# A fused gated attention and SwiGLU kernel: pieces of h ahead of other loads, one store behind them, and another mix of work slots

## Chip, cores and metric

The kernel runs on one NeuronCore of a Trainium2 chip. TensorE (PE) multiplies matrices, ScalarE (ACT) applies functions, VectorE (DVE) and GpSimd (POOL) work element by element, and SyncE (SP) issues most DMAs. The engines run beside one another and wait for each other by semaphores; each of them, and SP's queue of DMA issues, works through its own list in the order in which the program wrote it. The metric is the device time of one execution in microseconds; a smaller one is better. The kernel before takes 1419.05 us, the median of 3 runs (1418.94 to 1419.2).

## The reference

All arrays are float32; x has 2048 rows of 512. Attention has 32 heads of 16 columns, and the SwiGLU part an inner width of 1792. A sigmoid of one number per row mixes the two results.

```python
g = sigmoid((x * gate_w).sum(-1, keepdims=True))
# a: attention
q, k, v = (x @ wqkv) split into 32 heads of 16
p = softmax(q k^T / 4)               # 2048 x 2048 for each head
a = (p v, heads side by side) @ wo
# b: SwiGLU
h = silu(x @ w1) * (x @ w3)          # 2048 x 1792
b = h @ w2
out = g * a + (1 - g) * b
```

## The kernel before

**Products in three parts.** A float32 operand is split into a high part in the format fp32r and a low part that holds the rest. A product is the sum of high by high, high by low and low by high. The splitting is a cast and a subtraction: for weights and for h both are done by GpSimd (`halves_of`, lines 483 to 489), which reads a loaded tile ("fr" or "sg") and writes a pair of tiles. Such a call is one DMA on SP's queue and two GpSimd instructions. There are three "fr" buffers, three "raw", two each of "sg", "fh1", "fl1", "fh3" and "fl3", one "gw" and one "hx".

**Prologue and end.** The prologue turns x round, makes v for all rows and the first quarter of q and k, and takes about 85 us. At the end, behind the main loop, the last heads are divided by their sums and the second half of the output is made.

**The main loop** (lines 762 to 788) reads a string of letters, written ahead of time, and writes one piece of work for each letter. TensorE runs them in this order.
- *Q*: the scores of one unit, which is 128 keys by 512 queries for two heads (two matmuls of 512 columns, lines 736 to 747), and behind them the exp on ScalarE, of 128 x 1024 elements, into one of 8 tiles p. The scores have two buffers, so a Q slot can start only when ScalarE has read the scores of the Q slot two before it. 1024 Q slots in all.
- *P*: p by v for two units, eight matmuls of 512 columns (line 730).
- *F*: `feed`, which is filler: one matmul in each half of the array, for two blocks of other work at once (lines 409, 521 and 607 are the three kinds). A block that has run its matmuls in one half of the array runs them again in the other.

A *long* period (`one`) is eight Q, 20 F and four P, with the four P in one run at its end. A *short* period (`two`) is eight Q, 14 F and four P in two runs of two, with two Q between the runs. The string is 99 long periods, one lead-over, and 29 short ones, the last of which is cut at its end.

**The filler's blocks** come from `blocks` (lines 640 to 656) in this order: the other three quarters of q and k, and then w1 and w3 products for 14 slices f of h with four row blocks b each (136 blocks of 24 half slots, which make 1632 F slots); then h by w2 for 16 row tiles t (48 blocks of 28 half slots); then the output projection of the first six row tiles. The last two slices of h, f = 12 and 13, are taken in the order (12, 0), (12, 1), (13, 0), (13, 1), (12, 2), (13, 2), (12, 3), (13, 3). What the loop does not place is run behind it (line 798).

**h.** After a w1 product (`gate_done`) its result is copied, and ScalarE's exp of it is written at the next Q slot ahead of a P. The rest of the sigmoid, a sum, eight reciprocals of 64 columns and the final product, goes to a list `small`, of which each Q slot writes one or two steps on VectorE. The final product (`product`, lines 456 to 463) also stores the block to `h_d` in DRAM. For the w2 products h is read back by row tile: `load_piece(t, q)` (lines 497 to 503) reads rows 4q to 4q + 3 of slices for the 128 columns of tile t and splits them. Tile t has four pieces, q = 0 to 3, the last half as long; from t = 2 on a piece is written when its predecessor of tile t - 2 has been used for the last time. The w2 blocks (`load_w2`, lines 491 to 495) take the place of x in SBUF: block f goes to tiles that a row block of x had, so its cast waits until the last w1 and w3 products of that row block are done. w2 blocks 12 and 13 take the place of the last row block.

**The list `loads`** holds calls of `load_w2` and of `load_piece` for t = 0 and 1. A Q slot takes one of them, every second Q slot as long as `hurry` is false (which it is until the last w3 product), and each one after that (lines 779 and 780). As a slice is finished, calls are put at the list's end; the order in it is the order on SP's queue and on GpSimd:

```python
if f == NF - 1 and b == 0:
    loads.extend([lambda q=q: load_piece(0, q) for q in range(2)])
...
if (f, b) == (NF - 2, NB - 1):
    loads.extend([lambda q=q: load_piece(0, q) for q in (2, 3)])
if f == NF - 1:
    loads.extend([lambda c=c: load_w2(c) for c in range(4 * b, min(4 * b + 4, NF))])
```

Of the kernel before, what the change touches and what calls it, by code (L numbers as in the profile page):

```python
# [17 lines left out]
P = 128  # L18
# [5 lines left out]
NB = S // 512  # L24
NT = S // P
ND = D // P
NF = F // P
# [6 lines left out]
def gated_mix_kernel(ctx: ExitStack, tc: tile.TileContext, x, wqkv, wo, w1, w3, w2, gate_w, out):  # L34
# [18 lines left out]
    nc = tc.nc  # L53
# [16 lines left out]
    h_d = dram.tile([F, S], F32, name="h_d")  # L70
# [10 lines left out]
    def slot(tag, dtype=F32R, shape=(P, 512)):  # L81

        return (fw if tag[0] == "f" else fk).tile(list(shape), dtype, name=tag, bufs=BUFS.get(tag, 2))
# [185 lines left out]
    def load_step(s):  # L269
        half, j = divmod(s, NPAIR)  # L270
        load_q(j, half, s % 2)
        load_k(j, s % 2)
        load_guard(j, half, s % 2)
# [36 lines left out]
    def load_weights(chunk):  # L310
        out = []
        for n, w in zip("13", chunk["src"]):
# [5 lines left out]
            else:  # L318
# [7 lines left out]
    chunks = [dict(src=(wqkv[:, P * c:P * c + P], wqkv[:, D + P * c:D + P * c + P]), first=c == 1)  # L326
              for c in range(1, ND)]
# [74 lines left out]
    soon, later, small, stages, loads = [], [], [], [], []  # L402
    hurry = False
# [44 lines left out]
    def up_done(f, b):  # L448
        def done(ps):
            nonlocal hurry  # L450
            st = state[b]
            assert all(o["gone"] for o in state.values() if o is not st and o["last"])
            sg, gu = st["sg"], slot("hx" if st["last"] else "raw", F32)
            nc.vector.tensor_mul(gu, ps, st["gs"])

            def product():
                st["gone"] = True
                nc.vector.tensor_mul(sg, gu, sg)
                nc.sync.dma_start(h_d[P * f:P * f + P, 512 * b:512 * b + 512], sg)
                if f == NF - 1 and b == 0:  # L460
                    loads.extend([lambda q=q: load_piece(0, q) for q in range(2)])
                if f == NF - 1 and b == NB - 1:
                    loads.extend([lambda q=q: load_piece(1, q) for q in (2, 3)])

            if st["exp"]:
                small.append(product)
            else:
                st["up"] = product
            if (f, b) == (NF - 2, NB - 1):
                loads.extend([lambda q=q: load_piece(0, q) for q in (2, 3)])  # L470
            if f == NF - 1:
                loads.extend([lambda c=c: load_w2(c) for c in range(4 * b, min(4 * b + 4, NF))])
                if b == NB - 1:
                    loads.extend([lambda q=q: load_piece(1, q) for q in range(2)])
                    hurry = True
        return done
# [6 lines left out]
    def halves_of(src, hi, lo, tag):  # L483

        r = slot(tag, F32)
        n = hi.shape[-1]
        nc.sync.dma_start(r[:, 0:n] if len(src.shape) == 2 else r[:, 0:n].rearrange("p (f t) -> p f t", t=P), src)
        nc.gpsimd.tensor_copy(hi, r[:, 0:n])  # L488
        nc.gpsimd.tensor_sub(lo, r[:, 0:n], hi)  # L489

    def load_w2(f):
        if f % 4 == 0:
            w2H.append(xp.tile([P, 4, 512], F32R, name=f"xH{f // 4}"))
            w2L.append(xp.tile([P, 4, 512], F32R, name=f"xL{f // 4}"))
        halves_of(w2[P * f:P * f + P, :], w2H[-1][:, f % 4, :], w2L[-1][:, f % 4, :], "fr")

    def load_piece(t, q):
        hi, lo = (slot(SETS[t % 2][2 * q + i]) for i in range(2))
        tag = "fr" if t == 0 or t == 1 and q < 2 else "sg"
        n = min(4, NF - 4 * q)  # L500
        src = h_d[512 * q:512 * q + P * n, P * t:P * t + P].rearrange("(f p) t -> p f t", p=P)
        halves_of(src, hi[:, 0:P * n], lo[:, 0:P * n], tag)
        hs.setdefault(t, []).append((hi, lo))
# [72 lines left out]
    def divide(k, half):  # L576

        yield from reciprocals(k, half)
        for b in (2 * half, 2 * half + 1):
            for _ in range(5):  # L580
                yield
            if half == 0:
                o, r = slot("hx", F32), slot("gw", F32)
            else:
                both = wk.tile([P, 2, 512], F32, name="od")
                o, r = both[:, 0, :], both[:, 1, :]
            fetch_o(k, b, o, r)
            for _ in range(7):
                yield
            nc.gpsimd.tensor_mul(o, o, r)  # L590
            for _ in range(3):
                yield
            nc.sync.dma_start(N_d[P * k:P * k + P, 512 * b:512 * b + 512], o)
            yield
        if (k, half) == (2, 1):
            load_wo(2)
# [65 lines left out]
    lanes, ready, over = [None, None], ([], []), []  # L662
# [18 lines left out]
    def feed(rest=REST, gap=GAP):  # L681
        did = 0
        for lane in range(2):
            if lanes[lane] is None:
                lanes[lane] = pick(lane, rest, gap)
        for lane in range(2):
            t = lanes[lane]
            if t is None:
                continue
            product, done, length = t["block"]  # L690
            did += 1
            second = t["turn"] is not None
            ins = product(t["ps"], slice(64 * lane, 64 * lane + 64), t["n"], second)
            if second and t["n"] == 0:
                after(ins, t["turn"])
            t["n"] += 1
            if t["n"] == length:
                lanes[lane] = None
                if second:
                    done(t["ps"])  # L700
                    over[t["id"]] = clock
                else:
                    turn = nc.vector.memset(tick[:, 0:1], 0.0)  # L703
                    after(turn, ins)
                    t.update(n=0, turn=turn, since=clock)
                    ready[1 - lane].append(t)
        return did
# [18 lines left out]
    def pv(two):  # L726
        for j, half, k, gq, n, p in two:
            for h in range(2):
                r = 32 * (2 * gq + h)
                nc.tensor.matmul(acc[r:r + DH + 1, :], V[:, k, 2 * j + h, :], p[:, h, :],  # L730
                                 start=k == 0, stop=k == NT - 1)
            free.append(n)
        if k == NT - 1:
            evac(j, half)

    def score(j, half, k, gq):
        i = (NPAIR * half + j) % 2
        ps = psum2()
        t = 512 * gq
        for h in range(2):  # L740
            r = 64 * h
            nc.tensor.matmul(ps[:, h, :], Kt[i][r:r + 50, P * k:P * k + P],  # L742
                             Qt[i][r:r + 50, t:t + 512], start=True, stop=True)
        n = free.pop(0)
        p = wk.tile([P, 2, 512], F32, name=f"p{n}")
        nc.scalar.activation(p, ps, AF.Exp, scale=SCALE)  # L746
        return j, half, k, gq, n, p
# [3 lines left out]


    NP = 8
    LONG, SHORT = 99, 29
    one = "QQFFFFF" + "QFFF" * 5 + "QPPPP"
    two = "QFFF" * 4 + "QFFQPPQQPP"
    order = one * LONG + "QQFFF" + two * (SHORT - 1) + "QFFF" * 4 + "QPPQPP"
    free = list(range(NP))

# [1 line left out]
    pend, issued, clock = [], 0, 0  # L761
    for i, c in enumerate(order):
        clock += 1 if c != "P" else 4
        if c == "Q":
            step = issued // 32 + 1
            if issued % 32 == 6 and step < 2 * NPAIR:
                assert 8 * (ND - 1) - qk_left >= 8 * min(step // 4, ND - 1)
                load_step(step)
            pend.append(score(*next(units)))
            issued += 1  # L770
            while soon and order[i + 1] == "P":
                soon.pop(0)()
            if issued % 128 == (40 if issued // 128 == 5 else 12) and 1 <= issued // 128 < 8:
                stages.append(divide((issued // 128 - 1) % 4, (issued // 128 - 1) // 4))
            if small or later and hurry:
                for _ in range(3 if hurry else 1 + (len(small) > (6 if len(over) < 8 * len(chunks) - 16 else 0))):
                    if small or later and hurry:
                        (small or later).pop(0)()
            if loads and (hurry or issued % 2):
                loads.pop(0)()  # L780
            for stage in stages[:1]:
                if next(stage, stages) is stages:
                    stages.pop(0)
        elif c == "F":
            feed()
        else:
            pv(pend[:2])
            pend = pend[2:]
# [78 lines left out]
```

## Time and profile before

| | before |
|---|---|
| median of 3 runs | 1419.05 us (1418.94 to 1419.2) |
| profiled execution | 1419.72 us |
| its span, first to last instruction | 1417.9 us |
| mean granted TensorE clock | 0.997 |
| TensorE busy | 1407.5 us (99%) |
| ScalarE busy | 1022.8 us (72%) |
| VectorE busy | 484.0 us (34%) |
| GpSimd busy | 318.5 us (22%) |
| 16 DMA engines | 141.44 MB moved, 39.2% busy by SP's queue |

Times in rows of the profile are microseconds from the first instruction, unless marked ns. A row of the timeline has start, length, engine, line, operation, tiles written and read, shape and count; in brackets stand the idle time ahead of it and what ended that. Matmuls are pipelined and their ends are modelled: a row's length is not its price, the distance to the next row's start is. PEld is TensorE's loading of weights, which runs beside its matmuls. A row of the waits has the waiting engine and line, what it waited for, the total, the number of waits and the longest. SPq is SP's queue of DMA issues; a row of it that is long is one that stood and waited. The chain is the work that ended last, followed back from the end.

### The profile page before, as it was taken

Reading aid. Unit: us, or ns where it says so; the run is one execution under the profiler, and the core shown is the slowest. Engines: PE = TensorE matmul, PEld = TensorE weight load, DVE = VectorE, ACT = ScalarE, POOL = GpSimd, SP = SyncE. Lnnn points to the kernel's source line nnn. Section 1 sums busy time; section 2 is a strip of 40 time slices with the busy share of each in tenths; the row PEclk is TensorE's granted clock in tenths of the full one; section 3 lists DMA queues with packets and bytes.
Section 4 is the critical chain, followed back from the end, with each engine's and each line's share of the span. In section 5 each row is a group of like instructions: output and inputs, shape, how many; then the busy total and the mean of one; then the engine's idle time right before and its main releaser. Section 6 shows DMA issues by size and latency. Waiting matters only on the chain.

```text
span 1417.9 us, 28858 instructions
## 1 busy us (share of the span) xinstructions
PE 1407.5 (99%) x11399; PEld 809.7 (57%) x11399; DVE 484.0 (34%) x1067; ACT 1022.8 (72%) x1153; POOL 318.5 (22%) x356
## 2 busy tenths in 40 slices
PE   9999999999999999999999999999999999999998
PEld 7865555555555556555555555555555555555546
DVE  4421111554546445554454544531111101110113
ACT  4547777787777777777777777766777788888880
POOL 5023433110011011101110111553333422223130
PEclk9999999999999999999999999999999999999999
DMA  7554344333213333332233433444443443444435
GB/s 197 145 126 119 117 124 126 92 98 76 60 52 81 88 70 76 78 81 79 53 82 71 106 76 81 120 107 115 116 98 87 110 93 74 96 110 117 99 116 176
DMA packets 112671, 141.44 MB, mean 100 GB/s; under 512 B 16400, under 2 KB 70672, under 8 KB 109456
## 3 DMA queue, kind: packets, MB, share of 16 engines
q1 hardware_dynamic: 110384, 135.72, 39.2%
q10 hardware_dynamic: 2144, 3.80, 0.8%
q8 instruction: 92, 1.51, 0.5%
q14 instruction: 51, 0.42, 0.1%
HBM read 90.70 MB, written 48.76 MB: 98 GB/s over the span
## 4 chain that ended last, share of the span: by engine, by line
PE 93%; POOL 0%; DMA 0%; DVE 0%; issue 0%; ACT 0%; SPq 0%; ACTq 0%; POOLq 0%
PE acc L730 32%; PE f L409 27%; PE S L742 20%; PE f L521 11%; PE f L607 1%; PE f L95 0%; PE f L96 0%; PE f L97 0%; PE S L95 0%; PE S L97 0%; PE S L96 0%; DMA fr<-in_B_w_dram 0%; ACT p L746 0%; POOL xL L489 0%; POOL raw L489 0%
## 5 line engine op out<-in xcount | busy, mean ns | idle before, releaser
L746 ACT ACTIVATE p<-S 128x1024 f32<-128x1024 f32 x1024 | 957.6, 1045 | 319.7 <-PE S L742 319.3
L730 PE MATMUL acc<-p,V 128*17 128x512 f32 x4096 | 470.4, 594 | 0.0
L742 PE MATMUL S<-Qt,Kt 50*128 50x512 f32 x2048 | 414.6, 417 | 1.2 <-SPq L278 0.6
L742 PEld LDWEIGHTS S<-Qt,Kt 50*128 50x128 f32 x2048 | 183.8, 184 | 226.2 <-ACT p L746 85.4
L730 PEld LDWEIGHTS acc<-p,V 128*17 128x17 f32 x4096 | 104.5, 97 | 271.8 <-issue 266.5
L440 DVE RECIPROCAL sg<-sg 128x64 f32<-128x64 f32 x448 | 208.7, 517 | 38.0 <-issue 35.6
L409 PE MATMUL f<-xL,fh 64*128 64x512 f32 x1024 | 205.9, 392 | 0.0
L409 PE MATMUL f<-xH,fh 64*128 64x512 f32 x1024 | 205.8, 392 | 0.0
L409 PE MATMUL f<-xH,fl 64*128 64x512 f32 x1024 | 205.7, 391 | 0.0
L321 POOL CAST fh<-fr 128x512 fp32r<-128x512 f32 x32 | 20.8, 650 | 423.5 <-DMA fr<-in_B_w_dram 374.7
L409 PEld LDWEIGHTS f<-xH,fh 64*128 64x128 f32 x1024 | 98.9, 186 | 16.3
L409 PEld LDWEIGHTS f<-xH,fl 64*128 64x128 f32 x1024 | 98.9, 186 | 16.0
L409 PEld LDWEIGHTS f<-xL,fh 64*128 64x128 f32 x1024 | 98.8, 186 | 16.1
L703 DVE MEMSET tick<- 1x1 f32 x190 | 11.2, 59 | 262.4 <-PE f L521 130.9
L521 PE MATMUL f<-xL,fh 64*128 64x512 f32 x224 | 68.3, 399 | 0.0
L521 PE MATMUL f<-xH,fh 64*128 64x512 f32 x224 | 65.6, 399 | 2.7 <-POOL fh L488 2.7
L521 PE MATMUL f<-xH,fl 64*128 64x512 f32 x224 | 67.0, 399 | 0.0
L432 DVE COPY gs<-f 128x512 f32<-128x512 f32 x56 | 38.6, 689 | 79.9 <-PE f L409 77.7
L540 DVE SCALAR_TENSOR_TENSOR y<-f,omg,y 128x512 f32<-128x512 f32 x32 | 24.1, 752 | 118.1 <-PE f L521 118.1
L438 DVE TENSOR_SCALAR sg<-sg 128x512 f32<-128x512 f32 x56 | 27.8, 496 | 94.6 <-ACT sg L437 93.3
L521 PE MATMUL f<-xH,raw 64*128 64x512 f32 x192 | 58.2, 391 | 0.0
L711 DVE COPY u<-acc 128x512 f32<-128x512 f32 x32 | 22.1, 692 | 92.8 <-PE acc L730 87.3
(217 smaller groups left out, 1353.1 us busy)
## 6 DMA issues: line engine op xcount, KB each, us to landing
Kt<-kH_d SPq DMA_DIRECT2D x128, 128.0 KB
h_d<-sg SPq DMA_DIRECT2D x56, 256.0 KB
sg<-h_d SPq DMA_DIRECT2D x43, 256.0 KB
fr<-in_B_w_dram SPq DMA_DIRECT2D x42, 256.0 KB
Qt<-qH_d SPq DMA_DIRECT2D x128, 64.0 KB
Kt<-kL_d SPq DMA_DIRECT2D x64, 128.0 KB
fr<-in_A_wqkv_dram SPq DMA_DIRECT2D x18, 256.0 KB
Qt<-qL_d SPq DMA_DIRECT2D x64, 64.0 KB
```

The source lines that it names most:

```text
L321: nc.gpsimd.tensor_copy(wh, r)
L409: return nc.tensor.matmul(ps, w[i == 2][r, k, :], (xL if i == 1 else xH)[b][r, k, :], start=n == 0 and not second, stop=n == 3 * ND - 1 an ...
L432: nc.vector.tensor_copy(gs, ps)
L438: small.append(lambda: nc.vector.tensor_scalar(sg, sg, 1.0, None, op0=OP.add))
L440: small.append(lambda q=q: nc.vector.reciprocal(sg[:, q:q + 64], sg[:, q:q + 64]))
L521: ins = nc.tensor.matmul(ps, hs[t][q][i == 2][r, P * o:P * o + P], (w2L if i == 1 else w2H)[q][r, o, :], start=n == 0 and not second, stop ...
L540: nc.vector.scalar_tensor_tensor(y, ps, omg[:, t:t + 1], y, op0=OP.mult, op1=OP.add)
L607: return nc.tensor.matmul(ps, ot[t][i == 2][r, P * k:P * k + P], wo_[k][i == 1][r, :], start=n == 0 and not second, stop=n == 3 * ND - 1 a ...
L711: nc.vector.tensor_copy(u, acc)
L730: nc.tensor.matmul(acc[r:r + DH + 1, :], V[:, k, 2 * j + h, :], p[:, h, :], start=k == 0, stop=k == NT - 1)
L742: nc.tensor.matmul(ps[:, h, :], Kt[i][r:r + 50, P * k:P * k + P], Qt[i][r:r + 50, t:t + 512], start=True, stop=True)
L746: nc.scalar.activation(p, ps, AF.Exp, scale=SCALE)
```

## The change

It has three parts.
- The calls of `load_piece(0, ...)` are put at the front of `loads` and not at its end. The store of the last h block (f = 13, b = 3) is no longer written at once but put at the end of the list; the calls that follow it there, pieces (1, 2) and (1, 3), follow it still.
- From block 125 of the 136 on, each Q slot takes a load from the list, not every second one.
- The string has 78 long periods and 50 short ones in place of 99 and 29. A long period has 21 F, the added one behind the first two Q; a short one has 15 F, the added one ahead of the last Q before the first P run. In all there are 2388 F in place of 2387.

```diff
             def product():
                 st["gone"] = True
                 nc.vector.tensor_mul(sg, gu, sg)
-                nc.sync.dma_start(h_d[P * f:P * f + P, 512 * b:512 * b + 512], sg)
+                store = lambda: nc.sync.dma_start(h_d[P * f:P * f + P, 512 * b:512 * b + 512], sg)
+                if f == NF - 1 and b == NB - 1:
+                    loads.append(store)
+                    loads.extend([lambda q=q: load_piece(1, q) for q in (2, 3)])
+                    return
+                store()
                 if f == NF - 1 and b == 0:
-                    loads.extend([lambda q=q: load_piece(0, q) for q in range(2)])
-                if f == NF - 1 and b == NB - 1:
-                    loads.extend([lambda q=q: load_piece(1, q) for q in (2, 3)])
+                    loads[0:0] = [lambda q=q: load_piece(0, q) for q in range(2)]
...
             if (f, b) == (NF - 2, NB - 1):
-                loads.extend([lambda q=q: load_piece(0, q) for q in (2, 3)])
+                loads[0:0] = [lambda q=q: load_piece(0, q) for q in (2, 3)]
...
-    LONG, SHORT = 99, 29
-    one = "QQFFFFF" + "QFFF" * 5 + "QPPPP"
-    two = "QFFF" * 4 + "QFFQPPQQPP"
+    LONG, SHORT = 78, 50
+    one = "QQFFFFFF" + "QFFF" * 5 + "QPPPP"
+    two = "QFFF" * 5 + "QPPQQPP"
     order = one * LONG + "QQFFF" + two * (SHORT - 1) + "QFFF" * 4 + "QPPQPP"
...
-            if loads and (hurry or issued % 2):
+            if loads and (hurry or issued % 2 or len(over) > 8 * len(chunks) - 12):
                 loads.pop(0)()
```

## The prediction

> **What bounds the kernel now.** I read the page's sums and chain first, then who waited for whom, then TensorE's instructions in order of time around one period of each kind, around the one long wait, and at the end.
>
> ```profile
> span 1417.9 us, 28858 instructions
> PE 1407.5 (99%) x11399; PEld 809.7 (57%) x11399; DVE 484.0 (34%) x1067; ACT 1022.8 (72%) x1153; POOL 318.5 (22%) x356
> PE 93%; POOL 0%; DMA 0%; DVE 0%; issue 0%; ACT 0%; SPq 0%; ACTq 0%; POOLq 0%
> PE f L521 <- POOL fh L488: 2.7, 1, 2.7
> PEld S L742 <- ACT p L746: 85.4, 229, 0.9
> ```
>
> TensorE is the bound from end to end: 93% of the chain, and one wait of it over 2 us. So the time is the sum of what the written order makes TensorE do, plus that wait. The sum comes from the starts of the P runs (window of TensorE's timeline; a run cut by a window shows fewer instructions, its start is what counts):
>
> ```profile
> 91.88 3.63 PE L730 MATMUL acc<-p,V 128*17 128x512 f32 x32
> ...
> 930.13 1.05 PE L730 MATMUL acc<-p,V 128*17 128x512 f32 x8
> 940.49 3.63 PE L730 MATMUL acc<-p,V 128*17 128x512 f32 x32
> 956.90 3.63 PE L730 MATMUL acc<-p,V 128*17 128x512 f32 x32
> ...
> 1122.41 1.91 PE L730 MATMUL acc<-p,V 128*17 128x512 f32 x16
> ...
> 1371.91 1.91 PE L730 MATMUL acc<-p,V 128*17 128x512 f32 x16
> ```
>
> The first and the 82nd long period's runs start at 91.88 and 930.13: 81 periods, **10.349 us** each, for 20 F slots. The first and 28th short period's at 1122.41 and 1371.91: 27 periods, **9.241 us** each, for 14. The long period between 940.49 and 956.90 took 16.41, which is **6.06** too much. From 956.90 to 1122.41 lie 15 long periods and the one that leads over, which leaves 10.28 for the latter.
>
> **One period from inside.** Long, then short:
>
> ```profile
> 302.35 0.73 PE L742 MATMUL S<-Qt,Kt 50*128 50x512 f32 x4
> ...
> 303.86 0.40 PE L409 MATMUL f<-xL,fh 64*128 64x512 f32 x2
> 304.09 0.44 PE L742 MATMUL S<-Qt,Kt 50*128 50x512 f32 x2
> 304.37 0.39 PE L409 MATMUL f<-xH,fl 64*128 64x512 f32 x2
> ...
> 308.82 0.40 PE L742 MATMUL S<-Qt,Kt 50*128 50x512 f32 x2
> 309.15 3.63 PE L730 MATMUL acc<-p,V 128*17 128x512 f32 x32
> 312.70 0.73 PE L742 MATMUL S<-Qt,Kt 50*128 50x512 f32 x4
> ```
> ```profile
> 304.04 0.19 PEld L742 LDWEIGHTS S<-Qt,Kt 50*128 50x128 f32 x2 [0.22 <-ACT p L746]
> ```
> ```profile
> 1205.19 0.46 PE L742 MATMUL S<-Qt,Kt 50*128 50x512 f32 x2
> 1205.57 1.91 PE L730 MATMUL acc<-p,V 128*17 128x512 f32 x16
> 1207.42 0.73 PE L742 MATMUL S<-Qt,Kt 50*128 50x512 f32 x4
> 1208.07 1.91 PE L730 MATMUL acc<-p,V 128*17 128x512 f32 x16
> 1209.92 0.50 PE L742 MATMUL S<-Qt,Kt 50*128 50x512 f32 x2
> ```
>
> From 304.37 to 308.82 start 19 slots (15 F, 4 Q): **0.234 us** a slot. Two slots are longer. The third Q of the long period takes 0.28 (304.09 to 304.37): its weights are loaded at 304.04, released by ScalarE's exp, which frees the score banks; this is 0.05 over. The last Q of the short period takes 0.38 to the P run against 0.33 in the long one (308.82 to 309.15): again 0.05.
>
> **The wait.** TensorE, then its granted clock in that window, then the queue of SP, VectorE and GpSimd ahead of it:
>
> ```profile
> 946.31 0.38 PE L521 MATMUL f<-xL,fh 64*128 64x512 f32 x1
> 949.38 0.79 PE L521 MATMUL f<-xH,fh 64*128 64x512 f32 x1 [2.68 <-POOL fh L488]
> ```
> ```profile
> 949.40:956.30 6.90, 6.90 (x34) 5.21 (x36) 0.06 (x1) 3.25 (x4) 6.66 (x7) 0.54 0.19 57
> ```
> ```profile
> 927.68 12.13 SPq L459 DMA_DIRECT2D h_d<-sg  x2
> 939.91 0.88 SPq L487 DMA_DIRECT2D fr<-in_B_w_dram  x2
> ```
> ```profile
> 938.03 0.69 DVE L454 TENSOR_TENSOR hx<-f,gs 128x512 f32<-128x512 f32 x1 [1.35 <-PE f L409]
> 938.76 0.69 DVE L458 TENSOR_TENSOR sg<-hx,sg 128x512 f32<-128x512 f32 x1
> ```
> ```profile
> 942.98 0.61 POOL L488 CAST xH<-fr 128x512 fp32r<-128x512 f32 x1 [9.49 <-DMA fr<-in_B_w_dram]
> ...
> 944.90 0.61 POOL L488 CAST xH<-fr 128x512 fp32r<-128x512 f32 x1
> ...
> 946.82 0.61 POOL L488 CAST raw<-sg 128x512 fp32r<-128x512 f32 x1
> ...
> 948.72 0.61 POOL L488 CAST fh<-fr 128x512 fp32r<-128x512 f32 x1
> ```
>
> The last w3 product ends at about T = 938.0. VectorE makes the last h block by 939.45; SP has stood at its store since 928, so the last two w2 blocks are asked for at 939.91 and GpSimd begins on them at T + 5.0. Three items of 1.92 us stand ahead of piece (1, 0): its cast is done at 949.33, TensorE wanted it at 946.31 + 0.23 = T + 8.5. Afterwards TensorE runs on a clock of 0.54 for 6.9 us. Wait and slow clock are the 6.06.
>
> **The change, part by part.**
>
> *The store behind the w2 blocks.* SP no longer stands there; the two w2 DMAs wait for buffers alone (three "fr", freed by GpSimd one period earlier) and are issued several us before T. Their casts overwrite the last x block, so GpSimd can start at T at the earliest. In the new list pieces (1, 0), (1, 1) come ahead of the store and of piece (2, 0): two items stand ahead, not three. Cast done: T + 0.2 + 2 x 1.92 + 0.65 = T + 4.7. Wanted: the same 14 F slots lie between; by my count of the order, 4 single Q slots, the last Q (0.33), 1.85 + 0.65 + 1.85 for PP QQ PP (starts at 1205.57 to 1209.92) and the Q behind it (0.33) make T + 3.28 + 0.94 + 0.33 + 4.35 + 0.33 = T + 9.2. Margin 4.5 us. If something else still kept GpSimd from starting before T + 5.0, the cast would be done at T + 9.5: 0.3 late. The bounds are a gain of 6.06 and a remaining wait of 0.3; I take 6.06, since the queue that SP stood in is visible. Next in line: piece (1, 1), whose buffer GpSimd frees at T + 2.2 and whose first use is 8 F slots after (1, 0); not late. The store itself (block b = 3) is read from the 13th row tile on; nothing waits.
>
> *Pieces (0, 0), (0, 1) to the front:* two DMAs, four GpSimd instructions pass three w2 blocks (5.8 us on GpSimd). Both are first used 105 F slots later: nothing. *(0, 2), (0, 3) to the front:* the list is empty then. But (0, 3) now stands behind the store of block (12, 3) on SP, which waits for VectorE's reciprocals; its first use is 42 F slots later (over 20 us at 21 slots per 10.5), so nothing.
>
> *A load with each Q slot from block 125 on:* GpSimd needs 1.92 per load, Q slots are 0.94 apart, so SP will stand at "fr" buffers. Behind it are h stores and the next step's 14 K and Q DMAs, due 26 Q slots on (at 9.4 us per 8: 30 us). Nothing.
>
> *The order.* Long: one F more, 0.234, but it goes ahead of the third Q, whose 0.05 of waiting it covers: 10.349 + 0.234 - 0.05 = 10.533. Short: the F goes ahead of the last Q, same cover: 9.241 + 0.234 - 0.05 = 9.425. The bounds for each are 0.184 (covered) and 0.234 (not); I take the first, as the wait has a releaser in the row. A short period costs 9.241 - (10.349 - 6 x 0.234) = 0.30 more than a long one for the same F work; there are 21 more. That is the price of the change, 6.2 us, and it is in the sum. h work now runs at 15 slots per 9.4 us and not at 20 per 10.3, so its loads have more time.
>
> *The end.* Filled F slots are 2388 in both, by the counters of the loop. Before, four slots near the end find no block and five are run after the last P:
>
> ```profile
> 1382.59 2.22 PE acc L730 x16
> 1384.80 1.36 PE f L607 x5
> ```
> ```profile
> 1405.74 0.69 DVE L835 TENSOR_TENSOR p<-fr,p 128x512 fp32r<-128x512 f32 x1 [0.70 <-ACT p L834]
> ```
> ```profile
> 1408.15 0.39 PE L95 MATMUL S<-wo,p 128*128 128x512 f32 x1
> ```
>
> Afterwards none is left: 1.36 less behind the last P. The other branch (last store, division, split) is ready at 1406.43, TensorE comes to it at 1408.15, so 1.72 can be gained there and all of the 1.36 is. The slots move into the last short period, where Q slots wait for exps; 12.90 from 1371.91 to the last P's end becomes about 13.07.
>
> **Sum.** 91.88 + 0.18, plus 77 x 10.533 = 811.04, plus 10.28 + 0.18, plus 48 x 9.425 = 452.40, plus 13.07, plus 33.09 - 1.36 (1417.9 - 1384.81 is 33.09): **1410.8 of span, 7.1 less**. The profiled execution took 1419.72, its span and 1.8; the median is 1419.05, so I forecast **1411.9** for the median.
>
> **Rivals.** *A rest of the wait stays* (GpSimd starts no earlier than T + 5.0): 0.3, and if the clock falls as after the wait shown, 3.4 with it (half of 6.9): 1415.6. If all came back, 1418.0. For it: three engines in a row; against: the margin of 4.5. The Trainium skill (TensorE: Matmul & The Clock Gate, Part 1) has the clock drop only after an idle window of about 3.4 us; by that rule 0.3 would cost 0.3, 1412.2 (an estimate). Here the clock fell after 2.68, so I keep the dearer price.
>
> *The sixth F is not covered:* the 0.05 belongs to the Q slot and stays with it. 128 periods x 0.05 = 6.4: 1418.3, no change. Against: the row's releaser; for: 0.05 is near what the rows resolve. The same page (The mechanism) has weight loads run beside matmuls only in other row groups, which would make the load itself the bare part and give this time. The trace disagrees: the load at 304.04 runs beside the F of 303.86 (0.40 long) in both halves.
>
> *Slower:* with 21 F a block ends every 6.0 us and not 6.2, and blocks of 12 slots now meet the P run in other places; where VectorE comes late to a finished bank, TensorE waits for its copy.
>
> ```profile
> L432 DVE COPY gs<-f 128x512 f32<-128x512 f32 x56 | 38.6, 689 | 79.9 <-PE f L409 77.7 <-issue 2.0
> ```
>
> One copy of 0.69 laid bare in every fourth long period is 20 x 0.69 = 13.5: 1425.4. It decides (over 0.2% slower) from 15 such waits. Against: VectorE waited for TensorE, 77.7 of 79.9 us, not the other way.
>
> **Chances.** Forecast 0.70, a rest of the wait 0.10, not covered 0.08, slower 0.12. About 0.2% (2.8 us) is what a measurement here tells from no change: faster 0.77 (the forecast, most of the first rival), same 0.12, slower 0.11. The forecast's own range is 1410.2 (the 0.05 being 0.06, both ends) to 1413.5; the first rival takes it to 1416.5, which leaves out 2 in 10.
>
> **What would show it.** Long periods of 10.53 and short ones of 9.42 between P runs; a third Q of 0.23; no wait of TensorE for fh and a clock of 1.0 throughout; GpSimd's (1, 0) cast as third item, done some 4 us ahead of use; nothing of L607 after the last P. Long periods of 10.58 would speak for the second rival, a TensorE wait for VectorE between 100 and 900 us for the third, a clock of 0.5 near 900 us for the first.

## The result, and the profile after

The changed kernel takes 1412.85 us, the median of 6 runs (1409.74 to 1415.43). The kernel before took 1418.85 beside it (1418.56 to 1419.2, 6 runs). The ratio is 0.9957, with a 95% interval of 0.9944 to 0.997: faster by 6.0 us. The forecast was 1411.9, its range 1410.2 to 1416.5. The executions of the new kernel lie 5.7 us apart, those of the old one 0.6; that was not foreseen, and most of the experiments are about it.

The profiled execution is the fastest of the six, 1409.74, with a span of 1408.0 and a clock of 1.000. Its sums, its chain and TensorE's four longest waits:

```profile
span 1408.0 us, 28877 instructions
PE 1399.5 (99%) x11399; PEld 826.9 (59%) x11399; DVE 483.3 (34%) x1067; ACT 1033.5 (73%) x1153; POOL 318.7 (23%) x356
PE 93%; DVE 0%; POOL 0%; DMA 0%; issue 0%; ACT 0%; DVEq 0%; POOLq 0%; ACTq 0%
```
```profile
PE acc L334 <- DVE acc L330: 1.6, 1, 1.6
PE f L96 <- POOL fl L199: 0.9, 1, 0.9
PE S L745 <- DVE V L392: 0.7, 1, 0.7
PE f L409 <- DVE tick L706: 0.5, 1, 0.5
```

The wait of 2.7 us for fh is gone. The first three waits here lie ahead of the first P run. The fourth is new: TensorE waits for VectorE, inside the loop. It is the prediction's own sign for the third rival. The tick that it waits for is a write of one element, by which VectorE passes a block from one half of the array to the other.

The starts of P runs, from TensorE's timeline (a run cut by a window shows fewer instructions):

```profile
91.78 1.48 PE L733 MATMUL acc<-p,V 128*17 128x512 f32 x12
176.48 1.05 PE L733 MATMUL acc<-p,V 128*17 128x512 f32 x8
900.42 1.05 PE L733 MATMUL acc<-p,V 128*17 128x512 f32 x8
910.76 1.91 PE L733 MATMUL acc<-p,V 128*17 128x512 f32 x16
1363.21 0.62 PE L733 MATMUL acc<-p,V 128*17 128x512 f32 x4
1373.96 2.29 PE L733 MATMUL acc<-p,V 128*17 128x512 f32 x16
```

From 176.48 to 900.42 lie 69 long periods: 723.94 / 69 = **10.492 us** each, 10.533 predicted. From 910.76 to 1363.21 lie 48 short ones: **9.426** each, 9.425 predicted. The first eight long periods, 91.78 to 176.48, take 84.70, where eight of 10.492 are 83.94: 0.76 more, all of it in one. The last P run ends at 1373.96 + 2.29 = 1376.25, and 31.75 us follow to the end of the span; 31.73 were predicted.

Inside a long and a short period, the third Q and the last Q:

```profile
307.94 0.39 PE L745 MATMUL S<-Qt,Kt 50*128 50x512 f32 x2
308.17 0.39 PE L409 MATMUL f<-xH,fh 64*128 64x512 f32 x2
```
```profile
1202.59 0.40 PE L745 MATMUL S<-Qt,Kt 50*128 50x512 f32 x2
1202.92 1.91 PE L733 MATMUL acc<-p,V 128*17 128x512 f32 x16
```

The third Q takes 0.23 (0.28 before), the last Q of the short period 0.33 (0.38 before): both waits for the exp are covered.

The transition, from SP's queue, GpSimd, VectorE and TensorE:

```profile
899.40 2.95 SPq L490 DMA_DIRECT2D fr<-in_B_w_dram  x2
...
912.52 0.46 SPq L459 DMA_DIRECT2D h_d<-sg  x1
```
```profile
909.49 0.62 POOL L491 CAST xH<-fr 128x512 fp32r<-128x512 f32 x1 [6.29 <-PE f L409]
910.19 1.84 POOL L492 TENSOR_TENSOR xL<-fr,xH 128x512 fp32r<-128x512 f32 x1
911.97 0.60 POOL L491 CAST xH<-fr 128x512 fp32r<-128x512 f32 x1
...
913.88 0.61 POOL L491 CAST fh<-fr 128x512 fp32r<-128x512 f32 x1
```
```profile
910.19 0.69 DVE L458 TENSOR_TENSOR sg<-hx,sg 128x512 f32<-128x512 f32 x1
```
```profile
918.47 0.39 PE L524 MATMUL f<-xH,fh 64*128 64x512 f32 x1
```

T is 909.46 here. SP asked for the last two w2 blocks at 899.40, ten us ahead of it. GpSimd now waits for TensorE, not for a DMA, and starts at T. Piece (1, 0) is third in line, done at 914.49 = T + 5.0 (T + 4.7 predicted), and TensorE uses it at 918.47 = T + 9.0 (T + 9.2 predicted).

The new wait is in the long period between the P runs at 154.73 and 165.99, where the filler still makes q and k. TensorE, VectorE, GpSimd and SP there:

```profile
162.05 0.51 PE L409 MATMUL f<-xH,fh 64*128 64x512 f32 x2 [0.47 <-DVE tick L706]
```
```profile
161.31 0.69 DVE L420 COPY gs<-f 128x512 f32<-128x512 f32 x1 [6.90 <-DMA kL_d<-gs]
161.94 0.06 DVE L706 MEMSET tick<- 1x1 f32 x1
```
```profile
152.94 0.61 POOL L321 CAST fh<-fr 128x512 fp32r<-128x512 f32 x1 [9.46 <-PE S L745]
...
156.79 0.61 POOL L421 CAST sg<-gs 128x512 fp32r<-128x512 f32 x1
...
158.70 0.61 POOL L421 CAST sg<-gs 128x512 fp32r<-128x512 f32 x1
```
```profile
158.78 0.34 SPq L172 DMA_DIRECT2D kL_d<-gs  x1
```

Read from below: a finished k or q block is copied by VectorE to "gs" (two buffers), split by GpSimd and stored. Here two weight casts (L321) stand ahead of the splits in GpSimd's order, the first held up until 152.94. So the splits start at 156.79, the store of the low part is issued at 158.78, and VectorE, which needs that buffer for its next copy, is released at 161.31. The tick of another block stands behind that copy in VectorE's order, and TensorE can't go on with that block ahead of it.

### The profile page after: what moved, and what is told of

It reads as the page before. It is cut to its first block, busy times and chain, and to the rows that moved or that the text cites. A ratio compares the mean times of both kernels' runs of the same rounds, so it can differ in the third digit from the quotient of the medians.

```text
span 1408.0 us, 28877 instructions
## 1 busy us (share of the span) xinstructions
PE 1399.5 (99%) x11399; PEld 826.9 (59%) x11399; DVE 483.3 (34%) x1067; ACT 1033.5 (73%) x1153; POOL 318.7 (23%) x356
## 4 chain that ended last, share of the span: by engine, by line
PE 93%; DVE 0%; POOL 0%; DMA 0%; issue 0%; ACT 0%; DVEq 0%; POOLq 0%; ACTq 0%
PE acc L733 33%; PE f L409 27%; PE S L745 20%; PE f L524 11%; PE f L610 1%; PE f L95 0%; PE f L96 0%; PE f L97 0%; PE S L97 0%; PE S L96 0%; PE S L95 0%; DMA kL_d<-gs 0%; DVE V L392 0%; POOL gs L422 0%; ACT p L749 0%
## 5 line engine op out<-in xcount | busy, mean ns | idle before, releaser
L749 ACT ACTIVATE p<-S 128x1024 f32<-128x1024 f32 x1024 | 967.9, 1025 | 300.7 <-PE S L745 300.7
L745 PE MATMUL S<-Qt,Kt 50*128 50x512 f32 x2048 | 408.3, 411 | 1.0 <-DVE V L392 0.7
L409 PE MATMUL f<-xL,fh 64*128 64x512 f32 x1024 | 205.1, 391 | 0.0
L321 POOL CAST fh<-fr 128x512 fp32r<-128x512 f32 x32 | 19.9, 621 | 427.9 <-DMA fr<-in_B_w_dram 335.0
L524 PE MATMUL f<-xL,fh 64*128 64x512 f32 x224 | 64.6, 390 | 0.0
L432 DVE COPY gs<-f 128x512 f32<-128x512 f32 x56 | 38.7, 691 | 69.6 <-PE f L409 63.3
```

Of the source, the lines that this page charges most:

```text
L321: nc.gpsimd.tensor_copy(wh, r)
L409: return nc.tensor.matmul(ps, w[i == 2][r, k, :], (xL if i == 1 else xH)[b][r, k, :], start=n == 0 and not second, stop=n == 3 * ND - 1 an ...
L432: nc.vector.tensor_copy(gs, ps)
L524: ins = nc.tensor.matmul(ps, hs[t][q][i == 2][r, P * o:P * o + P], (w2L if i == 1 else w2H)[q][r, o, :], start=n == 0 and not second, stop ...
```

## The experiments

Times are medians. The first four ran on one chip beside a median of 1419.23 of the kernel before, the next four on one beside 1418.91, the last two beside 1418.74. Periods, waits and rows are those of each kernel's profiled execution.

**The changed kernel once more** (no edit).

> The changed kernel once more. Its six times lie between 1409.7 and 1415.4 us, those of the kernel before within 0.7. Theory: a wait of TensorE for VectorE in the q and k blocks (0.77 us at 160 us in the execution profiled) is longer in other executions, since it hangs on the landing of a store, and brings a slow clock with it: this profile shows a wait in the same stretch, 90 to 260 us, and the times spread again over 3 us or more, median 1411 to 1414. Rival: the spread is from the place near 900 us where the work turns from w1 and w3 to w2; then a wait for a piece of h is seen there in some execution.

Measured: 1412.63 (1411.23 to 1414.98), ratio 0.9955 (0.9942 to 0.9969), so time and spread repeat. Its profile has the new wait at 1.38 us: that period takes 12.17 us instead of 10.49. The same wait was 0.47 in the profile above (the expectation's 0.77 is what that period is longer, 11.26 against 10.49). So its length changes from execution to execution of one program. What sets it is the first weight cast. Here it starts only as the DMA of the weights lands:

```profile
154.16 0.61 POOL L321 CAST fh<-fr 128x512 fp32r<-128x512 f32 x1 [10.35 <-DMA fr<-in_A_wqkv_dram]
```

Counted from the first P run (92.11 here, 91.78 above) that is 0.89 us later than in the profile above, and the wait is 0.91 longer. In three runs further below with the same order and two buffers (the order alone, the last store written at once, the store moved behind alone) the cast is 1.56 to 1.81 later than above, and the wait 1.58 to 1.82 longer.

**The lists alone**, with the old order of slots:

```diff
-    LONG, SHORT = 78, 50
-    one = "QQFFFFFF" + "QFFF" * 5 + "QPPPP"
-    two = "QFFF" * 5 + "QPPQQPP"
+    LONG, SHORT = 99, 29
+    one = "QQFFFFF" + "QFFF" * 5 + "QPPPP"
+    two = "QFFF" * 4 + "QFFQPPQQPP"
```

> The list part alone (pieces to the front, last store behind, a load with each Q slot from block 125), with the old 99 and 29 periods. Forecast's theory: the wait for piece (1, 0) goes, since SP no longer stands at the store and GpSimd starts on the w2 blocks at about T + 0.2 and not T + 5.0; three items stand ahead of it still (piece (2, 0) is among them with this order), cast done at T + 6.6, wanted at T + 8.5. 6.1 us less than before: 1412.8. First rival (GpSimd starts no earlier): the wait stays, 1418.9.

Measured: 1413.7 (1413.5 to 1414.32), ratio 0.9959 (0.9946 to 0.9973), 0.9 over what was expected. No wait for fh, a clock of 1.0, long periods of 10.346, no wait near 160 us and executions within 0.8 us. GpSimd starts on w2 at 938.32, as the last w3 product ends. This part gains 5.5 us; the wait and its slow clock were 6.06.

**The order alone**, with the old lists and store (the diff of the change, without its edits of `loads` and `store`).

> The order part alone (78 periods of 21, 50 of 15), with the old lists and the old store. Forecast's theory: long periods of 10.50 to 10.53 us and short ones of 9.42, and the store still holds SP, so GpSimd starts at about T + 5.0; two items stand ahead of piece (1, 0), which is wanted at T + 9.2: a wait of 0.3 us, with or without a slow clock, so 0.3 to 3.7 us over the changed kernel's time, 1413 to 1416.5. If the order alone takes the wait away, the list part is worth nothing here: time of the changed kernel.

Measured: 1414.67 (1413.19 to 1416.78), ratio 0.9966 (0.9954 to 0.9978). Long periods 10.49, short ones 9.43. At the transition GpSimd starts at 917.16, released by the w2 DMA, and TensorE waits 0.39 for fh and 0.39 for fl; the stretch between two P runs there takes 8.48 us, 6.92 elsewhere. The clock of this profile stays at 1.0. Near 160 us it has the new wait, at 2.16. So the new wait comes with the order of slots, not with the lists. And the order alone makes the old wait small: the gains of the two parts (4.6 and 5.5) add up to more than the whole, since both take the same 6 us.

**The sixth F moved to the place of no cover**, ahead of the last Q of the long period:

```diff
-    one = "QQFFFFFF" + "QFFF" * 5 + "QPPPP"
+    one = "QQFFFFF" + "QFFF" * 4 + "QFFFFQPPPP"
```

> The changed kernel with the 21st F of a long period moved from behind the first two Q to the end of the period, ahead of the last Q but behind the third. Forecast's theory (the F covers the third Q's wait for an exp): the third Q takes 0.29 us again, the long period is 0.05 to 0.06 longer, 78 periods make 4 to 4.5 us: about 1417. Second rival (the 0.05 belongs to the slot): long period and time as in the changed kernel, within 1 us.

Measured: 1421.81 (1420.71 to 1422.93), ratio 1.0016 (1.0007 to 1.0025): 9 us slower than the kernel it was made from. The third Q is back at 0.29, the long period takes 10.587:

```profile
304.79 0.46 PE L745 MATMUL S<-Qt,Kt 50*128 50x512 f32 x2
305.08 0.39 PE L409 MATMUL f<-xH,fl 64*128 64x512 f32 x2
```

77 x (10.587 - 10.492) = 7.3 us. So where the F stands is worth 0.095 a period: the second rival (not covered) describes this kernel and not the changed one. The expectation had 0.05 to 0.06. By the means over some 60 periods of both profiles, the third Q is 0.056 of the 0.095; the rest lies in the other slots, an F taking 0.2334 on average and not 0.2317, and why is not shown. By the profiled spans the two kernels lie 13.1 us apart: 7.3 from this, and most of the rest from the wait in the q and k blocks, which moved to 146 us and grew; the two periods there take 15.36 and 11.67. No weight cast stands ahead there. The store of the low part is issued at 138.58, behind the K and Q loads of the next step in SP's queue, and VectorE's copy is released by it only at 145.79, 7.2 us later, where it was 2.5 in the changed kernel. The copy, the wait, and the clock, from a table of windows (the number before the last two is the granted clock in full speeds):

```profile
145.79 0.69 DVE L420 COPY gs<-f 128x512 f32<-128x512 f32 x1 [5.14 <-DMA qL_d<-gs]
```
```profile
146.54 0.79 PE L409 MATMUL f<-xH,fh 64*128 64x512 f32 x2 [2.87 <-DVE tick L706]
```
```profile
145.80:152.60 6.80, 6.06 (x28) 2.96 (x32) 0.74 (x3) 2.05 (x2) 1.89 (x2) 0.50 0.47 141
```

The wait began at 143.67. From 145.80 on, 0.7 us before it ended, the clock was at half, for some 6.8 us in all. That is how such a wait can cost more than itself.

**A third buffer "gs"** in the changed kernel:

```diff
-    BUFS = {"fr": 3, "raw": 3, "gw": 1, "hx": 1}
+    BUFS = {"fr": 3, "raw": 3, "gw": 1, "hx": 1, "gs": 3}
```

> The kernel after with a third gs buffer, so that VectorE's copy of a finished q or k block no longer has to wait until the store of the block two before it has landed. Theory (the wait near 160 us, VectorE late because a store of k or q is late, is what lifts the median over the best execution and spreads the times): no wait of TensorE for VectorE over 0.5 us between 90 and 180 us, the first eight long periods 83.9 us together (84.7 in the profile of after), median 1409 to 1410, spread under 1 us. Rival (the spread has another place): the first eight periods change, but the median stays at 1412 to 1413 with executions from 1410 to 1415.

Measured: **1409.99** (1409.73 to 1410.27, five runs), ratio 0.9937 (0.9923 to 0.9951). The first eight long periods take 83.93 us. VectorE at the place of the new wait:

```profile
160.29 0.69 DVE L420 COPY gs<-f 128x512 f32<-128x512 f32 x1 [5.40 <-PE f L409]
161.88 0.06 DVE L706 MEMSET tick<- 1x1 f32 x1 [0.89 <-PE f L409]
```

It is now released by TensorE's own matmul, and its tick waits for TensorE, not TensorE for the tick. The weights are late here too:

```profile
155.22 0.61 POOL L321 CAST fh<-fr 128x512 fp32r<-128x512 f32 x1 [11.27 <-DMA fr<-in_A_wqkv_dram]
```

Counted from the first P run (92.26) this cast is 1.80 later than in the changed kernel's profile, as late as in the run with a wait of 2.29, and TensorE does not wait. Median and spread both fall as the theory said: the wait on the store takes 2.6 to 2.9 us from the median of the changed kernel (1412.63 and 1412.85 against 1409.99) and makes its spread. This version beats both kernels.

**The old form for the first 14 long periods**, to take the wait away by another road:

```diff
-    LONG, SHORT = 78, 50
+    LONG, SHORT = 80, 48
-    order = one * LONG + "QQFFF" + ...
+    order = ("QQFFFFF" + "QFFF" * 5 + "QPPPP") * 14 + one * (LONG - 14) + "QQFFF" + ...
```

> The kernel after, but its first 14 long periods have the old form with 20 F, and there are 80 long and 48 short ones, so that the F slots come out nearly even. The same theory by another way: the q and k blocks end where they did before, GpSimd's weight casts and VectorE's copies meet as before, no wait near 160 us; 14 periods of 10.35 and 66 of 10.49, two short ones of 9.43 fewer and two long ones more. Median 1409 to 1410.5, spread under 1 us. Rival (the spread has another place): median 1412 to 1413, spread as after.

Measured: 1415.26 (1413.66 to 1416.83), ratio 0.9975 (0.9966 to 0.9984). The wait near 160 us is gone as expected: the first eight periods take 82.64, eight of 10.33. The time is a miss, since the shifted order brought two other costs. The last w3 product now ends inside a long period, and other loads stand in front (GpSimd, SP, TensorE):

```profile
920.02 0.61 POOL L491 CAST raw<-sg 128x512 fp32r<-128x512 f32 x1
...
927.70 0.61 POOL L491 CAST fh<-fr 128x512 fp32r<-128x512 f32 x1 [0.57 <-DMA fr<-h_d]
```
```profile
922.01 0.36 SPq L490 DMA_DIRECT2D sg<-h_d  x1
922.42 0.50 SPq L490 DMA_DIRECT2D fr<-h_d  x1
```
```profile
929.71 0.50 PE L524 MATMUL f<-xH,fl 64*128 64x512 f32 x2 [2.34 <-POOL fl L492]
```

A piece that goes through "sg" is third in GpSimd's line, the next "sg" load can be issued only as its split ends at 921.98, and the DMA behind it brings the late piece: TensorE waits 2.34 us. Besides, F blocks are left over again behind the last P run, and 33.30 us follow that run instead of 31.75. So this run supports the place of the new wait, says nothing of the spread, and shows that the margin at the transition belongs to one order of slots alone.

**The last store written at once**, with pieces at the front and a load with each Q slot as in the change:

```diff
+                store()
                 if f == NF - 1 and b == NB - 1:
-                    loads.append(store)
                     loads.extend([lambda q=q: load_piece(1, q) for q in (2, 3)])
-                    return
-                store()
```

> The kernel after, but the last h store is written at once as before; the pieces at the front and a load with each Q slot stay. Theory (the store on SP's queue is what holds the chain of loads up; the pieces at the front alone do not remove all of it): GpSimd's casts of pieces come 3 to 4 us later than in after, piece (1, 0) third in line, TensorE waits 0 to 1.6 us at the transition near 910 us, clock at 1.0; median 1412.5 to 1414.5. Rival (the pieces at the front are what counts): cast of piece (1, 0) done at least 2 us ahead of its use, no wait, time as after, 1412.6.

Measured: 1413.52 (1413.11 to 1416.86), ratio 0.997 (0.9959 to 0.9981). SP, GpSimd and TensorE at the transition (T is 911.33):

```profile
912.78 0.33 SPq L459 DMA_DIRECT2D h_d<-sg  x1
913.20 0.88 SPq L488 DMA_DIRECT2D fr<-in_B_w_dram  x2
```
```profile
916.53 0.61 POOL L489 CAST xH<-fr 128x512 fp32r<-128x512 f32 x1 [11.79 <-DMA fr<-in_B_w_dram]
...
920.39 0.62 POOL L489 CAST fh<-fr 128x512 fp32r<-128x512 f32 x1
```
```profile
921.06 0.50 PE L522 MATMUL f<-xH,fh 64*128 64x512 f32 x1 [0.32 <-POOL fh L489]
...
922.42 0.50 PE L522 MATMUL f<-xH,fl 64*128 64x512 f32 x1 [0.39 <-POOL fl L490]
```

This is the first rival's case, almost to the tenth: GpSimd starts at T + 5.2, the cast is done at T + 9.7, the wait for it is 0.32. That is 4.7 later than in the changed kernel, where 3 to 4 were expected. Its price was another: the stretch between the P runs takes 8.42 instead of 6.92, 1.50 us. The waits for the cast and for the low part are 0.71 of it; in the rest the matmuls of the two halves of the array, which start in pairs before, start apart. The clock stayed at 1.0. This profile also has the wait near 160 us, at 2.29.

**The store moved behind alone**, with the new order, pieces (0, q) at the end of the list and a load with every second Q slot:

```diff
-                loads[0:0] = [lambda q=q: load_piece(0, q) for q in (2, 3)]
+                loads.extend([lambda q=q: load_piece(0, q) for q in (2, 3)])
-            if loads and (hurry or issued % 2 or len(over) > 8 * len(chunks) - 12):
+            if loads and (hurry or issued % 2):
```

(and the same for pieces (0, 0), (0, 1)).

> The new order of slots with the store moved behind alone: pieces (0, q) at the end of the list as before, and a load with every second Q slot as before. Theory (the store decides): no wait for fh at the transition near 910 us, GpSimd starts on the w2 casts as the last w3 product ends, time as after, 1412 to 1413. Rival (the pieces at the front are needed too): the two w2 casts and the pieces ahead make the cast of (1, 0) late, a wait of 0.4 to 2.7 us near 917 us, 1413 to 1417.

Measured: 1413.44 (1411.59 to 1413.74), ratio 0.9959 (0.9945 to 0.9972). No wait at the transition; GpSimd starts at 912.59, as the last w3 product ends, and casts (1, 0) at 916.98, third in line. The wait near 160 us is there, at 2.05. Its time is somewhat over the 1412 to 1413 expected and is not told apart from that of the whole change. So the store is what decides there, and neither the pieces at the front nor the faster list is needed with this order.

**The third buffer in the kernel before**, and nothing else (the edit of "gs" above).

> The kernel before with a third gs buffer and nothing else. Theory (the wait near 160 us belongs to the new order; the old one has none there): no change, 1418.5 to 1419.3, ratio 0.999 to 1.001. Rival (a third buffer is worth something by itself, since k and q stores are late in the old order too): 1415 to 1417.

Measured: 1420.49 (1419.77 to 1421.44), ratio 1.0012 (1.0003 to 1.0021): no gain, some 1.7 us slower. The buffer is worth something only where the order of slots makes the store late. What the 1.7 us are was not settled; in its profile the loop starts 1.3 us later (first P run at 93.19, 91.88 before), and the wait for fh at the transition is 2.96 with the slow clock behind it.

**The third buffer with the new order and the old lists.**

> The kernel before with the new order of slots and the third gs buffer; lists and store as before. Theory: no wait near 160 us; at the transition GpSimd's cast of (1, 0) is late again and TensorE waits twice by about 0.4 us, 1.5 us in its period, without a slow clock; so 1.5 us over the kernel after with three buffers: 1411 to 1412, spread under 1 us. Rival (the wait at the transition brings the slow clock in some executions, as it did before): 1413 to 1416, spread of 2 us or more, mean clock under 0.998 in the long ones.

Measured: 1412.1 (1410.76 to 1412.72), ratio 0.9953 (0.9939 to 0.9966), spread 2.0. No wait near 160 us; at the transition the stretch takes 8.21, 1.3 us over, at full clock. The median is 2.1 over that of the whole change with three buffers, somewhat over the 1.5 expected, with nearly four times the spread.

## Why the prediction was right, point by point

**The wait.** Right, for the reason given: SP stood in its queue. The cast was done at T + 5.0, 0.3 over the forecast: one GpSimd subtraction took 1.84 us and not 1.28, and GpSimd started 0.2 earlier than in the sum. But either part would have taken most of the 6.06: with the old order the lists gain 5.5, and with the new order the old lists lose only 1.3 to 1.6 there and keep the full clock. So with the order in place, moving the store is worth some 1.5 us (by the medians 0.7 to 2.1). The prediction gave the whole 6.06 to the store; what holds is the sum of both parts.

**The order.** The long period came out at 10.492, 0.041 under the forecast: 77 x 0.041 = 3.2 us of gain that the sum lacks. The step that was mis-sized is "one F more, 0.234, but it goes ahead of the third Q, whose 0.05 of waiting it covers". By the mean over 65 periods of each profile, the third Q went from 0.292 to 0.230, 0.06 and not 0.05 (the range had allowed for 0.06); the other 0.03 are some 0.001 in each other slot, an F taking 0.232 on average instead of 0.233; why is not shown. The short period, 0.381 to 0.330 for its last Q and 9.426 in all, was right.

**The end.** Right: nothing is left behind the last P run, 31.75 against 31.73. The kernel with the old form of 14 periods shows the other case, with left-over blocks and 33.30.

**The sum.** Of the 2.8 us between the predicted span of 1410.8 and the 1408.0 measured, 3.2 are the long periods, 0.8 go the other way for the new wait, and 0.3 are an earlier first P run (91.78, predicted 92.06). Two figures of the prediction beside the sum are off: 20 x 0.69 is 13.8 and not 13.5, and 0.01 more in each of 125 periods makes a lower end of some 1410.65 and not 1410.2. Neither changes a conclusion.

**What was missed** is the third rival's mechanism, in another place: VectorE is late with a copy, and TensorE waits, here for the tick that stands behind the copy. The prediction looked for it in the 136 blocks of h, at one copy of 0.69 laid bare every fourth period, and argued from a row of those blocks (L432) alone. It came in the q and k blocks (L420), where a store's landing stands between, and ahead of the store the landing of the weights; it comes once and not 20 times, and costs the median 2.6 to 2.9 us. That the forecast is only 0.95 under the median is in part luck, as two misses nearly cancel: by its sum the profiled execution should have taken 1412.6 and took 1409.74, 2.9 less; and the median, expected 0.7 under the profiled execution, lies 3.1 above it, which is the wait in its longer forms.

Its own mechanism in the h blocks does occur once, near 828 us. Here it is in the run with the store alone (GpSimd, VectorE, TensorE):

```profile
826.34 1.29 POOL L322 TENSOR_TENSOR fl<-fr,fh 128x512 fp32r<-128x512 f32 x1
```
```profile
826.72 1.47 DVE L458 TENSOR_TENSOR sg<-raw,sg 128x512 f32<-128x512 f32 x1
828.11 0.68 DVE L432 COPY gs<-f 128x512 f32<-128x512 f32 x1
```
```profile
828.93 0.50 PE L409 MATMUL f<-xH,fh 64*128 64x512 f32 x2 [0.32 <-DVE tick L706]
```

That period took 11.08 and not 10.49. A product twice as long as usual pushed the copy back.

**Still open.** Why some executions of the changed kernel take 1413 to 1415 was not seen in a profile. The longest wait that a profile shows near 160 us is 2.29, at full clock; that is 1.8 more than in the execution of 1409.74, or some 1411.6 (an estimate). What makes the weights land later in one execution than in another is open too. Their mean clock is 0.998 or 0.999 in five cases of five, that of the six shorter ones 1.0; together with the half clock at the wait of 2.87 this speaks for waits long enough to bring the slow clock. It is argued and not shown, and a clock of 0.999 stands beside executions of 1410 us of the version with three buffers too. That the third buffer takes them away is shown.

## What to carry to other kernels

A change of a written order moves every meeting of the engines behind it, so the rows of *all* stretches have to be looked at, the short first one too: ask for each finished block which copy, which buffer, which store and which load stand between it and its next use. Two parts of a change that remove the same wait don't add up; cost each with the other already made. Filler is cheapest where it stands ahead of work that would wait anyway: one F moved within its period was worth 0.095 us of 10.5, and this 77 times, though only 0.056 of it is the wait that it covers.

## What the runs showed of the hardware

**VectorE and GpSimd hold each other up.** GpSimd's subtraction takes 1.28 to 1.30 us; begun at 910.19 together with VectorE's product of two SBUF operands (0.69) it took 1.84. Near 828 us it was the other way: VectorE's product began at 826.72, within GpSimd's subtraction (826.34 to 827.63), and took 1.47, about the 0.9 that the other still needed and 0.69 less a little. The Trainium skill (SBUF — State Buffer, Who interferes with whom) has the two share a port pair as an exclusive lock, for which a VectorE instruction with two SBUF inputs contends with a GpSimd instruction that reads SBUF; these rows agree with it.

**When the clock falls.** Waits of TensorE of 2.16 (the order alone), 2.29 (the last store written at once) and 2.34 us (the old form for 14 periods) left the clock at 1.0. At waits of 2.68 (before), 2.87 (the F without cover) and 2.96 (the third buffer in the kernel before) it fell to half while TensorE still waited, by narrow windows about 2.2, 2.1 and 2.7 us into the wait, and stayed there for some 6.8, 6.8 and 3.4 us. So the length of the wait alone does not settle it: it could fall 2.1 us into one wait and stay up through another of 2.34. The Trainium skill (TensorE: Matmul & The Clock Gate, Part 1) gives an idle window of about 3.4 us for this; here less was enough. The first rival's price for 0.3 us of waiting, 3.4 us of slow clock, was wrong: waits of 0.32 and 0.39 left the clock at 1.0.
